# Block passes over w1 with 512-column products, sums of weights for four steps at a time, and other PSUM banks

## The chip, the cores and the metric

The kernel runs on one core of one Trainium2 chip. The metric is device time in microseconds (us). The kernel before takes 515.64 us (median of 3 runs, 515.21 to 515.76).

## The reference

A transformer block on S = 2048 tokens with D = 512 channels: a linear-attention mixer, and then an MLP over the token axis. The change lies in the MLP:

```python
h  = x + attention(layernorm(x))
g  = layernorm(layernorm(h))            # (S, D)
u  = gelu(einsum("sd,sf->df", g, w1) + b1)   # w1 (2048, 1792)
y  = einsum("df,fs->ds", u, w2) + b2         # w2 (1792, 2048)
out = h + y.T
```

## The kernel before

**Passes and steps.** The hidden axis F = 1792 is cut into 7 passes of 256. Passes 0 and 1 are multiplied during the attention's last turns. From then on an explicit list, `STEPS`, orders the work: steps 0 to 7 are pass 2, a plain pass ("v"); steps 8 to 31 are passes 3, 4 and 5, the block passes ("u"); steps 32 to 39 are pass 6, plain again; steps 40 to 95 are w2's ("y"), seven steps for each pair of output tiles. A step of w1 takes two tiles of 128 tokens against 256 columns of w1.

**Block passes.** A plain step does four 128x128 blocks of weights against 512 columns, with three matmuls each: high part of the weights by high part of the data, high by low, low by high. A block step is a Strassen-like scheme with seven products (`P1` to `P7`) in place of eight. It needs, on 256 columns, sums of weight blocks (`w_sums`) and sums of data blocks (made by `h_ops`, split into high and low parts by `h_parts` into tiles named `cb`; step 8 + j uses data pair j).

**From weight to matmul.** For each step, SP loads raw blocks into one half of a double buffer (`BLOCK`, four steps in each half); DVE makes four sums in place (`w_sums`, L801 to L805); then `w_parts` splits the step's seven blocks: ACT copies them to the high part (L66, 128x896) and DVE subtracts that to get the low part (L67, 128x896). In w1's steps the parts of step n lie in one of three buffers, `ws[n % 3]`, so that the copy of step n + 3 has to wait until TensorE has finished step n. The loop calls `prepare(n + 2)` while step n is issued. Before, `w_sums` does two steps at a time in w1's passes, behind the parts of every even step m, for steps m + 2 and m + 3.

**Order.** From the attention's end on, ACT, DVE, POOL, PE and SP run in the order in which the code issues (`manual_schedule`). The calls put down with `at(n, ...)` come behind `prepare(n + 2)`, at half steps ahead of it: `h_sums` (four DVE adds for one data pair), `h_parts`, `u_adds` (ACT copies and accumulating DMAs that POOL issues, at the steps in `U_ADDS`), `u_parts` (ACT and DVE splits of a finished pass's u, for w2).

**Banks.** `ps_b` has four PSUM banks, `ps_f` and `ps_q` two each. Before, a block pass takes four banks (`four_banks`): pass 3 and 5 two of `ps_f` and two of `ps_q`, pass 4 four of `ps_b`; the plain pass 6 takes two of `ps_b`. `u_out` reads a finished pass out of its banks into u. The steps of w2 already use four products of 512 columns (`wide`) and three of 256 (`narrow`), in six banks.

Of the kernel before, what the change touches and what calls it, by code (L numbers as in the profile page):

```python
# [9 lines left out]
F32 = mybir.dt.float32  # L10
# [7 lines left out]
P = 128  # L18
# [24 lines left out]
def block_kernel(ctx: ExitStack, tc: tile.TileContext, x, xT, wT, phic, wo, w1, b1, w2, b2,  # L43
# [749 lines left out]
    def w_sums(g):  # L793

        if 2 * g >= len(STEPS) or STEPS[2 * g][0] == "v":
            return
        plain = STEPS[2 * g][0] == "y"
        raw = BLOCK[g // 2 % 2] if plain else RAW[g]
        added = ADDED(2 * g)
        if not added:  # L800
            nc.vector.tensor_add(raw[:, :, 0], raw[:, :, 3], raw[:, :, 1])  # L801
        nc.vector.tensor_add(raw[:, :, 5], raw[:, :, 0], raw[:, :, 2])
        nc.vector.tensor_add(raw[:, :, 6], raw[:, :, 4], raw[:, :, 5])
        if not added:
            nc.vector.tensor_add(raw[:, :, 1], raw[:, :, 1], raw[:, :, 2])  # L805
# [199 lines left out]

    def four_banks(i):
        return [new_bank(q) for q in ((ps_b,) * 4, (ps_f, ps_f, ps_q, ps_q))[i]]
# [7 lines left out]
    def firsts(banks):  # L1015
        a, b, c, d = banks
        tmp = wqp.tile([P, 4, HD], F32, name="tmp", tag="small")
        nc.scalar.activation(tmp[:, 1], a[:, 0], AF.Copy)
        nc.vector.tensor_sub(tmp[:, 2], a[:, 1], tmp[:, 1])
        nc.vector.tensor_sub(tmp[:, 3], tmp[:, 2], d[:, 0])  # L1020
        nc.vector.scalar_tensor_tensor(tmp[:, 0], b[:, 0], -1.0, tmp[:, 2], op0=ALU.mult, op1=ALU.subtract)
        return tmp[:, 0:2], tmp[:, 3].unsqueeze(1).to_broadcast([P, 2, HD])

    def u_out(p, banks):
        e, u3 = firsts(banks)
        U[p] = o = ur.tile([P, 4, HD], F32, name="u")
        nc.vector.tensor_add(o[:, 0:2], banks[1], u3)
        nc.vector.tensor_add(o[:, 2:4], banks[2], e)

# [11 lines left out]
    def wide_step(n, sp, p):  # L1041
        t = 2 * sp
        if p == 0:
            b3, b2 = [new_bank((ps_f, ps_q)[sp % 2]) for _ in range(2)]
            BK[:] = [new_bank(ps_b) for _ in range(4)] + [b3, b2]
# [46 lines left out]
    def last_step(n, sp, p):  # L1092
        t = 2 * sp
        if p == 0:
            b3, b2 = [new_bank((ps_f, ps_q)[sp % 2]) for _ in range(2)]
            BK[:] = [new_bank(ps_b) for _ in range(4)] + [b3, b2]
# [46 lines left out]
    def step(n):  # L1143

        kind, i, j = STEPS[n]
        if kind == "u":
            if j == 0:
                BANKS[0] = four_banks(i % 2)
            products(n, BANKS[0], lambda m: NB[j][m], j == 0, j == NT // 2 - 1)
# [4 lines left out]
        elif kind == "v":  # L1154
            if j == 0:
                PU[i] = [ps_b.tile([P, D], F32, name="pu", tag="pu") for _ in range(2)]
            wh_, wl_ = PARTS[n]
# [58 lines left out]
    def prepare(m):  # L1216
# [82 lines left out]
```

## Time and profile before

| what | value |
|---|---|
| time, median of 3 | 515.64 us |
| span of the profiled execution, first to last instruction | 513.1 us |
| PE busy in the span | 507.8 us (99%) |
| DVE, ACT, POOL busy | 438.4, 310.6, 261.1 us |
| block passes (steps 8 to 31), 288.47 to 348.94 us: DVE, ACT busy | 55.28, 37.70 us of 60.47 |
| granted TensorE clock | 1.000 |

The profiled execution has only its span; the time of a run is about 2.5 us longer than this (515.64 - 513.1), for what lies ahead of the first and behind the last instruction. In the rows of a timeline the first column is the start from the span's beginning, the second the duration (of a group: to the end of its last), and the brackets hold the engine's idle time just before and who ended it. A row "x9" is nine of the same kind in sequence.

### The profile page before, as it was taken

To read this page: it belongs to the slowest core of one execution; us is meant where nothing else is said; L and a number is where in the kernel's file an instruction comes from. 1 tells how busy PE (TensorE), PEld (TensorE's weight loads), DVE (VectorE), ACT (ScalarE), POOL (GpSimd) and SP (SyncE) were. 2 spreads that over 40 slices of the span, in tenths; PEclk is the share of its full clock that TensorE was granted. 3 is DMA by queue.
4 is the path that set the end of the run, shared out by engine and by line. 5 is a ranking of instruction groups with operands and counts; after the bars stand their busy time and mean duration, and the time that the engine had idled before them with its cause. 6 is when DMAs were issued, how large, how long until landed. Compare 5 with 4: busy or idle time off the path is not lost.

```text
span 513.1 us, 10496 instructions
## 1 busy us (share of the span) xinstructions
PE 507.8 (99%) x4024; PEld 441.7 (86%) x4024; DVE 438.4 (85%) x746; ACT 310.6 (61%) x557; POOL 261.1 (51%) x212
## 2 busy tenths in 40 slices
PE   8999999999999999999999999999999999999997
PEld 8888888888877777777788999998899999999997
DVE  6799889989887899699877898898799889868983
ACT  6999863525267878867676754577655444434530
POOL 3579997876999999985200421202323212211220
PEclk9999999999999999999999999999999999999999
DMA  8642301010123234354325775545677797668734
GB/s 308 217 144 84 103 22 42 1 65 21 42 64 103 67 100 145 127 169 132 95 69 185 150 159 125 133 115 151 173 164 147 181 199 167 122 153 190 169 51 85
DMA packets 53266, 63.35 MB, mean 123 GB/s; under 512 B 4832, under 2 KB 39904, under 8 KB 53216
## 3 DMA queue, kind: packets, MB, share of 16 engines
q1 hardware_dynamic: 44288, 51.90, 32.5%
q0 software_dynamic: 8640, 10.62, 14.9%
q8 instruction: 31, 0.51, 0.4%
q10 hardware_dynamic: 288, 0.17, 0.1%
q14 instruction: 19, 0.16, 0.1%
HBM read 48.39 MB, written 11.14 MB: 116 GB/s over the span
## 4 chain that ended last, share of the span: by engine, by line
PE 95%; DVE 2%; ACT 1%; DMA 1%; issue 0%; POOL 0%; DVEq 0%
PE py L989 25%; PE py L996 9%; PE pu L71 9%; PE pu L72 8%; PE pu L73 8%; PE py L998 4%; PE pk_ps L71 3%; PE pk_ps L72 3%; PE pk_ps L73 3%; PE pv L73 3%; PE pv L71 3%; PE pv L72 3%; PE po L71 3%; PE po L73 2%; PE po L72 2%; PE pn L616 2%
## 5 line engine op out<-in xcount | busy, mean ns | idle before, releaser
L66 ACT ACTIVATE wp<-wraw 128x896 fp32r<-128x896 f32 (+1 forms) x96 | 82.4, 895 | 68.3 <-DVE wraw L805 23.9
L67 DVE TENSOR_TENSOR wp<-wraw,wp 128x896 fp32r<-128x896 f32 (+1 forms) x96 | 95.5, 1019 | 14.9 <-ACT wp L66 14.6
L989 PE MATMUL py<-cb,wp 128*128 128x256 f32 x678 | 92.6, 283 | 0.0
L989 PEld LDWEIGHTS py<-cb,wp 128*128 128x128 f32 x678 | 86.1, 191 | 0.0
L1039 POOL DMA_DIRECT2D out<-u x28 | 24.8, 963 | 89.8 <-ACT u L1085 28.9
L951 POOL DMA_DIRECT2D tt<-u x14 | 13.4, 960 | 60.6 <-ACT tt L950 34.5
L490 POOL TENSOR_TENSOR ez<-eq,zB 128x1024 f32<-128x1024 f32 x16 | 38.4, 2406 | 3.8 <-ACT zB L550 3.8
L219 POOL TENSOR_TENSOR pk<-pk,sk 128x1024 f32<-128x1024 f32 x16 | 31.1, 1947 | 11.3 <-DVE sk L218 10.1
L996 PE MATMUL py<-cb,wp 128*128 128x512 f32 x126 | 36.1, 394 | 0.0
L514 POOL TENSOR_TENSOR eq<-eq,w 128x1024 f32<-128x1024 f32 x16 | 32.4, 2025 | 3.5 <-DVE w L511 3.5
L223 POOL TENSOR_TENSOR zacc<-zacc,pk 128x1024 f32<-128x1024 f32 x13 | 31.4, 2412 | 0.5
L989 PE MATMUL py<-hs,wp 128*128 128x256 f32 x216 | 30.0, 283 | 0.0
L989 PEld LDWEIGHTS py<-hs,wp 128*128 128x128 f32 x216 | 27.8, 192 | 0.1
L195 ACT ACTIVATE pk<-pk,r 128x1024 f32<-128x1024 f32 x16 | 18.4, 1149 | 15.0 <-DVE pk L173 14.4
L989 PE MATMUL py<-uf,wp 128*128 128x256 f32 x198 | 26.6, 283 | 0.0
L71 PE MATMUL pu<-wq,xs 128*128 128x512 f32 x64 | 26.1, 409 | 0.0
L71 PE MATMUL pu<-hs,whl 128*128 128x512 f32 x64 | 26.0, 406 | 0.0
L71 PE MATMUL po<-woh,oh 128*128 128x512 f32 x64 | 25.3, 396 | 0.1
L72 PE MATMUL pu<-wq,xs 128*128 128x512 f32 x64 | 25.0, 391 | 0.0
L73 PE MATMUL pu<-wq,xs 128*128 128x512 f32 x64 | 25.0, 390 | 0.0
L72 PE MATMUL pu<-hs,whl 128*128 128x512 f32 x64 | 25.0, 390 | 0.0
L73 PE MATMUL po<-woh,ol 128*128 128x512 f32 x64 | 25.0, 390 | 0.0
(226 smaller groups left out, 1422.1 us busy)
## 6 DMA issues: line engine op xcount, KB each, us to landing
wraw<-in_w SPq DMA_DIRECT2D x112, 256.0 KB, 3.4
out<-u POOLq DMA_DIRECT2D x21, 256.0 KB, 5.4
xraw<-in_xT SPq DMA_DIRECT2D x16, 256.0 KB, 2.9
xh<-in_x SPq DMA_DIRECT2D x16, 256.0 KB, 2.7
h<-in_x SPq DMA_DIRECT2D x16, 256.0 KB, 2.9
out<-h SPq DMA_DIRECT2D x16, 256.0 KB, 2.0
wraw<-in_wT SPq DMA_DIRECT2D x12, 256.0 KB, 4.9
tt<-u POOLq DMA_DIRECT2D x14, 128.0 KB, 3.8
```

The costliest lines, as they stand in the source:

```text
L66: nc.scalar.activation(hi, src, AF.Copy)
L67: lo_engine.tensor_sub(lo, src, hi)
L71: nc.tensor.matmul(o, ah, bh, start=first, stop=False)
L72: nc.tensor.matmul(o, ah, bl, start=False, stop=False)
L73: return nc.tensor.matmul(o, al, bh, start=False, stop=last).ins
L219: nc.gpsimd.tensor_mul(heads(PK[t]), heads(PK[t]), sk.unsqueeze(2).to_broadcast([P, 2 * H, DH]))
L223: nc.gpsimd.tensor_add(zacc, zacc, PK[t])
L490: nc.gpsimd.tensor_mul(EZ[t], EQ[t], zB)
L514: nc.gpsimd.tensor_mul(heads(EQ[t]), heads(EQ[t]), W[t].rearrange("p g c h -> p (g c h)").unsqueeze(2).to_broadcast([P, 2 * H, DH]))
L989: nc.tensor.matmul(o, w[:, m[0]], x[:, y], start=opens and i == 0, stop=closes and i == 2, skip_group_check=True)
L996: nc.tensor.matmul(o, wh_[:, m[0]], x(m[1]), start=first, stop=False, skip_group_check=True)
L1039: nc.gpsimd.dma_start(out[t * P:(t + 1) * P, k * HD:], flat(a), accum_op=ALU.add)
```

## The change

It does four things.

1. `products` (the block steps of w1) does P3, P2, P5 and P4 by `wide`: one matmul of 512 columns for the weights' high part (data high and low side by side) and one of 256 for the low part, 17 matmuls in place of 21. A pass now takes six banks (`six_banks`): always the four of `ps_b`, and two of `ps_q` (passes 3 and 5) or `ps_f` (pass 4). The order of the products differs in a pass's first, middle and last steps. `u_out` now has five ACT copies out of the banks (before: one) and nine DVE operations (before: five).
2. `w_sums` in w1's passes does four steps at a time, behind the parts of step m where m % 4 is 3, for steps m + 1 to m + 4 (those of steps 12 to 15 behind the parts of step 11, and so on).
3. The plain pass 6 takes `ps_f`; w2's pairs take `ps_q` and `ps_f` in the other order.
4. `U_ADDS` shifts eight calls of `u_adds` by a step (pass 0's last two, pass 1's last two, all of pass 2, one of pass 3), and the adds and parts of data pair 6 come a step later.

```diff
-        plain = STEPS[2 * g][0] == "y"
-        raw = BLOCK[g // 2 % 2] if plain else RAW[g]
+        raw = BLOCK[g // 2 % 2]
...
-    U_ADDS = {0: (5, 7, 9), 1: (6, 8, 10), 2: (11, 13, 15), 3: (19, 21, 23), 4: (28, 30, 32), 5: (34, 35.5, 37)}
+    U_ADDS = {0: (5, 8, 10), 1: (6, 9, 11), 2: (12, 14, 16), 3: (19, 21, 24), 4: (28, 30, 32), 5: (34, 35.5, 37)}
...
+    def six_banks(pool):
+        b3, b2 = [new_bank(pool) for _ in range(2)]
+        return [new_bank(ps_b) for _ in range(4)] + [b3, b2]
 
     def products(n, banks, x, first, last):
-        a, b, c, d = banks
-        for o, m, opens in ((a[:, 0], P1, True), (a[:, 1], P6, False), (d[:, 0], P7, True), (b[:, 0], P5, True),
-                            (b[:, 1], P4, False), (c[:, 0], P3, True), (c[:, 1], P2, False)):
-            narrow(o, n, m, x(m[1]), first and opens, last)
+        b16, b7, b5, b4, b3, b2 = banks
+
+        def singles():
+            narrow(b16[:, 0], n, P1, x(P1[1]), first, last)
+            narrow(b16[:, 1], n, P6, x(P6[1]), False, last)
+            narrow(b7[:, 0], n, P7, x(P7[1]), first, last)
+
+        w3, w2, w5, w4 = (b3, P3), (b2, P2), (b5, P5), (b4, P4)
+        if last:
+            singles()
+            wide(n, x, first, last, w5, w4)
+            wide(n, x, first, last, w3, w2)
+        elif first:
+            wide(n, x, first, last, w3, w2)
+            singles()
+            wide(n, x, first, last, w5, w4)
+        else:
+            wide(n, x, first, last, w3, w2, w5, w4)
+            singles()
...
+    def u_out(p, banks):
+        b16, b7, b5, b4, b3, b2 = banks
         tmp = wqp.tile([P, 4, HD], F32, name="tmp", tag="small")
+        u3, e0, e1, u2 = [tmp[:, k] for k in range(4)]
         U[p] = o = ur.tile([P, 4, HD], F32, name="u")
+        add, sub = nc.vector.tensor_add, nc.vector.tensor_sub
+        nc.scalar.activation(e1, b16[:, 0], AF.Copy)
+        for k, b in enumerate((b5, b4, b3, b2)):
+            nc.scalar.activation(o[:, k], b[:, 1], AF.Copy)
+        sub(u2, b16[:, 1], e1)
+        sub(u3, u2, b7[:, 0])
+        add(o[:, 0], b5[:, 0], o[:, 0])
...
-    for j, n in enumerate((0, 1, 2, 3, 5, 9, 12), 1):
+    for j, n in enumerate((0, 1, 2, 3, 5, 10, 12), 1):
...
-        elif m % 2 == 0 and m + 2 < Y0:
+        elif m % 4 == 3 and m + 1 < Y0:
             w_sums(m // 2 + 1)
```

How the rows of DVE stand at the first block pass. `wp<-wraw,wp` is the low part of one step, `wraw<-wraw` a sum of weights, `hf<-hf` the adds for a data pair, `cb_3571` the parts of data pair 6. Before, from the low part of step 10 on:

```order
L67 TENSOR_TENSOR wp<-wraw,wp 128x896
L801 TENSOR_TENSOR wraw<-wraw 128x2x128
L802 TENSOR_TENSOR wraw<-wraw 128x2x128
L803 TENSOR_TENSOR wraw<-wraw 128x2x128
L805 TENSOR_TENSOR wraw<-wraw 128x2x128
L67 TENSOR_TENSOR wp<-wraw,wp 128x896
L67 TENSOR_TENSOR cb_3571<-hf,cb_3571 128x4x256
L67 TENSOR_TENSOR wp<-wraw,wp 128x896
```

These are the low part of step 10, the sums for steps 12 and 13, the low part of 11, the parts of pair 6, the low part of 12. Now, from the low parts of steps 8 to 10 on:

```order
L67 TENSOR_TENSOR wp<-wraw,wp 128x896 x3
L738 TENSOR_TENSOR hf<-hf 128x256 x2
L739 TENSOR_TENSOR hf<-hf 128x256 x2
L67 TENSOR_TENSOR wp<-wraw,wp 128x896
L800 TENSOR_TENSOR wraw<-wraw 128x4x128
L801 TENSOR_TENSOR wraw<-wraw 128x4x128
L802 TENSOR_TENSOR wraw<-wraw 128x4x128
L804 TENSOR_TENSOR wraw<-wraw 128x4x128
L67 TENSOR_TENSOR wp<-wraw,wp 128x896
L67 TENSOR_TENSOR cb_3571<-hf,cb_3571 128x4x256
L738 TENSOR_TENSOR hf<-hf 128x256 x2
L739 TENSOR_TENSOR hf<-hf 128x256 x2
```

Between the low parts of steps 10 and 11 stand the adds of pair 6; between those of 11 and 12 stand the sums for steps 12 to 15, twice as wide; behind 12 come the parts of pair 6 and the adds of pair 7, and then the low part of step 13.

DVE at the end of that pass (step 15), now: the low part of step 15, the sums for steps 16 to 19, the low parts of 16 and 17, and the first four operations of `u_out`, which read the banks of pass 3 (`py`):

```order
L67 TENSOR_TENSOR wp<-wraw,wp 128x896
L800 TENSOR_TENSOR wraw<-wraw 128x4x128
L801 TENSOR_TENSOR wraw<-wraw 128x4x128
L802 TENSOR_TENSOR wraw<-wraw 128x4x128
L804 TENSOR_TENSOR wraw<-wraw 128x4x128
L67 TENSOR_TENSOR wp<-wraw,wp 128x896 x2
L1039 TENSOR_TENSOR tmp<-py,tmp 128x256
L1040 TENSOR_TENSOR tmp<-tmp,py 128x256
L1041 TENSOR_TENSOR u<-py,u 128x256
L1042 TENSOR_TENSOR u<-py,u 128x256
```

Before, the sums for steps 18 and 19 stood between the low parts of 16 and 17, and no matmul of step 16 wrote into a bank that `u_out` was still to read.

PE at the same seam, now, with what its rows wait for: the end of step 15 (first two rows), and step 16:

```order
L995 MATMUL py<-hs,wp 128x512 x2
L997 MATMUL py<-hs,wp 128x256 x2
L995 MATMUL py<-hs,wp 128x512 [waits Activation_49]
L995 MATMUL py<-hs,wp 128x512
L997 MATMUL py<-hs,wp 128x256 [waits DVE_49]
L997 MATMUL py<-hs,wp 128x256
L988 MATMUL py<-hs,wp 128x256 [waits DVE_49]
L988 MATMUL py<-hs,wp 128x256 x2
L988 MATMUL py<-cb_3447,wp 128x256 x3
L988 MATMUL py<-cb_3447,wp 128x256 [waits DVE_49]
```

The first 512-column matmul waits for ACT (the high part of step 16), the first with low weights (L997) for DVE (the low part), and the first of P1 (L988) for DVE again: it opens the bank that `u_out` reads with its first two operations.

More of the change, by code (lines that the diff above doesn't have):

```diff
@@ new lines, in u_out @@
+    def u_out(p, banks):
+        b16, b7, b5, b4, b3, b2 = banks
+        tmp = wqp.tile([P, 4, HD], F32, name="tmp", tag="small")
+        u3, e0, e1, u2 = [tmp[:, k] for k in range(4)]
+        U[p] = o = ur.tile([P, 4, HD], F32, name="u")
+        add, sub = nc.vector.tensor_add, nc.vector.tensor_sub
[5 more added lines that the diff above has]
+        add(o[:, 0], b5[:, 0], o[:, 0])
+        add(o[:, 1], b4[:, 0], o[:, 1])
+        nc.vector.scalar_tensor_tensor(e0, o[:, 0], -1.0, u2, op0=ALU.mult, op1=ALU.subtract)
+        add(o[:, 0], o[:, 0], u3)
+        add(o[:, 2], b3[:, 0], o[:, 2])
+        add(o[:, 3], b2[:, 0], o[:, 3])
+        add(o[:, 1:4], o[:, 1:4], tmp[:, 0:3])
@@ L1043, in wide_step @@
         if p == 0:
-            b3, b2 = [new_bank((ps_f, ps_q)[sp % 2]) for _ in range(2)]
+            b3, b2 = [new_bank((ps_q, ps_f)[sp % 2]) for _ in range(2)]
             BK[:] = [new_bank(ps_b) for _ in range(4)] + [b3, b2]
@@ L1094, in last_step @@
         if p == 0:
-            b3, b2 = [new_bank((ps_f, ps_q)[sp % 2]) for _ in range(2)]
+            b3, b2 = [new_bank((ps_q, ps_f)[sp % 2]) for _ in range(2)]
             BK[:] = [new_bank(ps_b) for _ in range(4)] + [b3, b2]
@@ L1147, in step @@
             if j == 0:
-                BANKS[0] = four_banks(i % 2)
+                BANKS[0] = six_banks((ps_f, ps_q)[i % 2])
             products(n, BANKS[0], lambda m: NB[j][m], j == 0, j == NT // 2 - 1)
@@ L1155, in step @@
             if j == 0:
-                PU[i] = [ps_b.tile([P, D], F32, name="pu", tag="pu") for _ in range(2)]
+                PU[i] = [(ps_f if i > PLAIN else ps_b).tile([P, D], F32, name="pu", tag="pu") for _ in range(2)]
             wh_, wl_ = PARTS[n]
```

13 lines of the change are left out of this document (removed).

## The prediction

> **What bounds the kernel now.** I read the page's busy shares first, then who waited for whom on PE, and then the chain that ended last.
>
> ```profile
> PE 507.8 (99%) x4024; PEld 441.7 (86%) x4024; DVE 438.4 (85%) x746; ACT 310.6 (61%) x557; POOL 261.1 (51%) x212
> PE pk_ps L357 <- DVE eps L62: 1.1, 1, 1.1
> PE pu L335 <- POOL ph L361: 0.4, 1, 0.4
> PE pn L616 <- DVE h L641: 0.2, 1, 0.2
> PE 95%; DVE 2%; ACT 1%; DMA 1%; issue 0%; POOL 0%; DVEq 0%
> ```
>
> The middle three rows are all the waits of PE: 1.7 us, none in the steps that change. So PE's own stream sets the time, and a change counts if it shortens that stream or puts a wait into it. The chain gives the block passes in one piece, and a middle step of w2 in three:
>
> ```profile
> 288.63 60.47 PE py L989 x504
> ...
> 397.00 1.07 PE py L989 x9
> 398.07 0.93 PE py L996 x4
> 399.00 0.47 PE py L998 x4
> ```
>
> 504 matmuls are 24 steps of 21: 120 ns each, 2.52 us per step, with no gap. w2's step, which has the new form already, takes 1.07 + 0.93 + 0.47 = 2.47 us.
>
> The second view is how full the other engines are there (columns: stretch, its length, then busy PE, PEld, DVE, ACT, POOL):
>
> ```profile
> 288.47:348.94 60.47, 60.47 (x505) 60.47 (x504) 55.28 (x92) 37.70 (x57) 13.84 (x16) 1.00 0.60 139
> 303.83 0.96 ACT L66 ACTIVATE wp<-wraw 128x896 fp32r<-128x896 f32 x1 [0.67 <-PE py L989]
> 306.35 0.95 ACT L66 ACTIVATE wp<-wraw 128x896 fp32r<-128x896 f32 x1 [1.56 <-PE py L989]
> 302.86 1.24 PE L989 MATMUL py<-hs,wp 128*128 128x256 f32 x9
> 305.38 1.24 PE L989 MATMUL py<-hs,wp 128*128 128x256 f32 x9
> ```
>
> DVE is busy for 91% of the block passes. The copies of steps 16 and 17 begin 0.25 us after steps 13 and 14 have ended (a step begins 0.72 us into a row of nine: 303.58, 306.10), because there are only three buffers of parts. So the parts can never be far ahead of PE, and DVE has little to catch up with.
>
> **What the change takes away.** Per step 0.05 us of PE, 24 times: 1.15 us. The Trainium skill, in "TensorE: Matmul & The Clock Gate", Back-to-back issue gap, prices a warm matmul at its columns over 2.4 GHz plus 2.5 ns; by that the twelve old and the eight new matmuls differ in four times 2.5 ns, 0.24 us in all, as an estimate. The rows disagree (120 ns for 256 columns, 0.93 / 4 = 233 ns for 512), and I go by them.
>
> **What it puts in.** Sums of four steps at a time exist in w2's part; there the rows show what follows them:
>
> ```profile
> 371.94 0.69 DVE L801 TENSOR_TENSOR wraw<-wraw 128x512 f32<-128x512 f32 x1
> ...
> 374.01 0.68 DVE L805 TENSOR_TENSOR wraw<-wraw 128x512 f32<-128x512 f32 x1
> 375.76 1.09 DVE L67 TENSOR_TENSOR wp<-wraw,wp 128x896 fp32r<-128x896 f32 x1 [1.07 <-ACT wp L66]
> 374.77 0.95 ACT L66 ACTIVATE wp<-wraw 128x896 fp32r<-128x896 f32 x1 [2.89 <-issue]
> ```
>
> Four sums take 2.75 us; the copy of the next step can begin only after them, and DVE stands idle for 1.07 us until its low part can follow. For two steps they took 1.68 us:
>
> ```profile
> 306.00 0.42 DVE L801 TENSOR_TENSOR wraw<-wraw 128x256 f32<-128x256 f32 x1
> ...
> 307.26 0.42 DVE L805 TENSOR_TENSOR wraw<-wraw 128x256 f32<-128x256 f32 x1
> ```
>
> They served steps further on, so that the next step's copy ran beside them. DVE thus saves 0.61 us for four steps and loses 1.07. In w2 more buffers cover that; in w1 nothing does. I follow DVE's rows in the new order from a place that stays as it was, the low part of step 10:
>
> ```profile
> 290.23 1.09 DVE L67 TENSOR_TENSOR wp<-wraw,wp 128x896 fp32r<-128x896 f32 x1 [0.37 <-ACT wp L66]
> 293.83 1.22 DVE L67 TENSOR_TENSOR cb<-hf,cb 128x1024 fp32r<-128x1024 f32 x1
> 297.56 0.88 DVE L738 TENSOR_TENSOR hf<-hf 128x256 f32<-128x256 f32 x2
> 298.47 0.89 DVE L739 TENSOR_TENSOR hf<-hf 128x256 f32<-128x256 f32 x2
> 299.27 2.08 DVE L67 TENSOR_TENSOR wp<-wraw,wp 128x896 fp32r<-128x896 f32 x2
> 308.60 0.42 DVE L1019 TENSOR_TENSOR tmp<-py,tmp 128x256 f32<-128x256 f32 x1
> ...
> 310.39 0.68 DVE L1028 TENSOR_TENSOR u<-py,tmp 128x512 f32<-128x512 f32 x1
> 302.45 0.40 ACT L950 ACTIVATE u<-u 128x256 f32<-128x256 f32 x1
> 288.47 0.52 PE L989 MATMUL py<-hs,wp 128*128 128x256 f32 x3
> ```
>
> Low 10 ends at 291.3. Adds of pair 6 (1.8 us): 293.1. Low 11 (1.0 behind other work): 294.1. Sums for 12 to 15 (2.75): 296.8. Copy, then low 12 (0.07 + 0.95, 0.03 + 1.09): 298.9. Parts of pair 6 (1.15): 300.0. Adds of pair 7: 301.7. Low 13: 302.7. PE begins step 8 at 288.47 and would begin step 12 at 298.36 and step 13 at 300.83. A middle step wants its low part 0.93 us after its start, behind its four 512-column products: 299.29 for step 12, met with 0.3 to spare; 301.76 for step 13, **missed by 1.0 us**, with 0.1 for the signal.
>
> On to the seam. Low 14: 303.7. Parts of pair 7: 304.8. Low 15: 305.8. Sums for 16 to 19: 308.5. Low 16: 310.6. Copy 17 stands behind two ACT copies of `u_adds` (0.3 each), so low 17 ends at 312.1. Only then comes `u_out`'s first subtraction (0.42): 312.4. Step 16 would begin at 309.25 and, 0.70 us later (two products of 512, two of 256), open the bank which that subtraction reads. It can at 312.5 in place of 309.95, **2.55 us** late. Before, passes alternated between banks, and nothing waited here.
>
> The same chain at the later places, with 2.47 us per step: step 18 begins at 316.75, `u_out` ends at 316.0, low 19 at 317.9, sums at 320.6, low 20 at 322.7 against 322.6 wanted: **0.2**. Copy 23 starts 0.25 behind step 20; low 23 ends at 326.7, sums 329.3, low 25 at 332.5, `u_out`'s first at 332.8 against 332.5: **0.4** at step 24's bank. Step 28 repeats step 20: **0.2**. Behind low 28 stand the parts of pass 0's u:
>
> ```profile
> 338.80 0.95 DVE L67 TENSOR_TENSOR cb<-tt,cb 128x768 fp32r<-128x768 f32 x1
> 339.66 2.09 DVE L67 TENSOR_TENSOR wp<-wraw,wp 128x896 fp32r<-128x896 f32 x2
> 341.67 1.22 DVE L67 TENSOR_TENSOR cb<-u,cb 128x1024 fp32r<-128x1024 f32 x1
> 362.58 1.83 DVE L67 TENSOR_TENSOR wp<-wraw,wp 128x896 fp32r<-128x896 f32 x2 [1.02 <-ACT wp L66]
> ```
>
> 1.22 + 0.95 more, so low 29 is **0.5** late. In plain pass 6, the third `u_out` (nine operations, 3.9 us by the 0.42 and 0.95 of these rows, for the 2.5 from L1019 to L1028) puts DVE back just ahead of the sums for step 40, which already end in a stand-still of 1.02 us; step 38 may lose **0.4** (0 to 0.8). The waits sum to 1.0 + 2.55 + 0.2 + 0.4 + 0.2 + 0.5 + 0.4 = 5.25 us. Less 1.15 that is **4.1 us more**: span 513.1 to 517.2. The time of a run is 2.5 us above the span, so 515.64 becomes **519.8 us**.
>
> **What I cost at nothing.**
>
> ```profile
> 387.53 0.38 ACT L1080 ACTIVATE u<-py 128x256 f32<-128x256 f32 x1 [0.67 <-PE py L998]
> 296.72 0.42 ACT L950 ACTIVATE tt<-wraw 128x256 f32<-128x256 f32 x1 [2.01 <-DMA wraw<-u]
> ```
>
> The four more copies of ACT per `u_out` (0.38 each, as in w2's steps) lie beside DVE, and ACT is busy for 37.70 of 60.47 us; uncovered they would cost 1.5 us per pass. The moved `u_adds` issue the same DMAs on POOL in nearly the same order, now behind other ACT copies; ACT's waits for landings were no wait of PE. Uncovered, a late one holds a copy by up to 2.0 us. Pass 6 in `ps_f` finds free banks as it did in `ps_b`; in `ps_b` it would now wait like step 16. SP's loads keep their order, each behind the low part eight steps earlier.
>
> **Rivals.**
>
> *The chain on DVE does not bind: faster.* If copies 12 and 16 ran beside the sums, as before, DVE would gain 1.07 us at each, and with 1.0 us less neither step 13 nor, mostly, the bank of step 16 would wait. Then only 1.15 us go: 514.5. It decides at 1.0 us of slack between low 10 and low 13. Against it stands the idle 1.07 in w2's row, on the same two lines. Chance 0.10.
>
> *Half of it.* The waits of step 13 and of the seam overlap more, or low parts are wanted later than I say, and 1 to 2.5 us of waits stay: 515.5 to 517.0. Chance 0.12, two thirds of it within 0.2% (1.0 us, about what a measurement of this kernel can tell from no change).
>
> *Only columns count.* Old and new forms stream the same 3072 columns for four products. If these set the pace, the 1.15 us don't come and the waits do: 520.9. w2's steps speak against it. Chance 0.06. The gap rule of the Trainium skill above is nearly this one; by it the time would be 520.6.
>
> *PE runs slowly after a wait.* At the start of the trace it does, for one kind of 128x128 fp32 matmul after another:
>
> ```profile
> L357 PE MATMUL pk_ps<-ones 128*128 128x128 f32 x18 | 3.7, 392 | 1.1 <-DVE eps L62 1.1
> L335 PE MATMUL pu<-ph,wraw 128*128 128x128 f32 x16 | 2.1, 285 | 0.4 <-POOL ph L361 0.4
> ```
>
> 3.7 / 18 = 206 ns each, then 131. A stretch of 3.7 us at that rate loses 3.7 x (1 - 131 / 206) = 1.35 us; after the waits of steps 16 and 13 it would be 521.1 to 522.5. Chance 0.07, since the single waits are short (1.0 and 1.6 us). The Trainium skill, same page, What's actually happening, says that the clock halves after about 3.4 us of idleness and comes back after as long a busy stretch; by it no wait here is long enough, and the first rows fit the second half of the rule.
>
> **Numbers.** Forecast 0.65, with a range of its own of 518.6 to 521.2 (seven waits, each 0.2 us uncertain for the signal and the weight load behind it, and 0 to 0.8 at step 38). Faster by over 0.2%: 0.10. Within: 0.07. Slower: 0.83. The range 516.5 to 522.5 leaves out the first rival, most of the second, and little above.
>
> **What would show it.** Right: rows of PE waiting for DVE `wp` L67 and for `tmp` L1039, the longest near 310 us; DVE idle for about 1.07 us ahead of the low parts of steps 12, 16, 20, 24, 28; no PE wait ahead of step 13; w2's steps and the granted clock as before. Wrong: block passes of 59.3 us without PE waits (first rival), or waits in other places, for ACT or for DMA.

## The result, and the profile after

The changed kernel takes **523.05 us** (median of 4 runs, 520.86 to 523.65) where the kernel before takes 515.70 beside it: ratio **1.0137, interval 1.0116 to 1.0157**. The forecast was 519.8. Its sign held, its size did not: 4.1 us were forecast and 7.35 came, above both ranges that went with the forecast (518.6 to 521.2, and 516.5 to 522.5). Of the four executions one kept the granted clock throughout (mean 1.000) and took 520.86 us; the other three, at a mean of 0.997, took 522.74 to 523.65. The profiled execution has a span of 521.0 us, 7.9 more than before. One execution of the kernel e13 below, 1287.12 us with every matmul slow, is left out of that kernel's ratio. Line numbers below are those of the kernel named; in the changed kernel the narrow products are L988 and the wide ones L995 and L997.

First the page of the changed kernel: PE's busy time, and the clock granted to it in 40 slices of the span.

```profile
PE 512.3 (98%) x3928; PEld 438.6 (84%) x3928; DVE 440.5 (85%) x734; ACT 312.9 (60%) x569; POOL 261.1 (50%) x212
PEclk9999999999999999999999998999999999999999
```

PE has 96 matmuls fewer and is busy 4.5 us longer. One slice of the clock shows an 8: something slowed the matmuls themselves, and no wait list can show that. The waits of PE and of its weight loads (in total, times, longest):

```profile
PE py L997 <- DVE wp L67: 1.7, 3, 1.0
PE py L988 <- DVE tmp L1039: 1.6, 2, 1.3
PE py L988 <- DVE u L1097: 0.4, 1, 0.4
PEld py L997 <- DVE wp L67: 3.3, 4, 1.4
```

Where the time went is read from stretches that are the same work in both kernels: the block passes, plain pass 6, and the first and second quarter of w2 (stretch, length, then busy PE, PEld, DVE, ACT, POOL and the clock). First the kernel before, whose block passes the prediction has shown (60.47):

```profile
348.94:370.73 21.79, 21.79 (x99) 18.03 (x97) 16.73 (x26) 14.60 (x28) 5.02 (x6) 1.00 0.60 146
370.73:406.38 35.65, 35.65 (x246) 33.13 (x245) 31.98 (x50) 18.90 (x33) 10.37 (x13) 1.00 0.81 179
406.38:441.93 35.55, 35.55 (x248) 33.07 (x246) 32.22 (x49) 16.31 (x26) 7.32 (x9) 1.00 0.74 160
```

The changed kernel:

```profile
288.90:355.21 66.31, 62.92 (x409) 56.47 (x408) 55.64 (x79) 39.77 (x68) 13.80 (x17) 0.97 0.55 128
355.21:377.40 22.19, 22.19 (x99) 17.87 (x97) 18.30 (x32) 13.92 (x29) 4.46 (x7) 1.00 0.58 139
377.40:413.35 35.95, 35.95 (x247) 33.26 (x245) 32.28 (x49) 20.29 (x35) 11.15 (x14) 1.00 0.75 174
413.35:449.80 36.45, 36.03 (x247) 33.20 (x246) 32.24 (x50) 16.28 (x26) 8.09 (x10) 1.00 0.78 166
```

The block passes take 5.84 us more, plain pass 6 takes 0.40, w2's first quarter 0.30, its second 0.90; the parts ahead of the block passes began 0.43 later, and the rest of w2 is the same to 0.02. The two places in the block passes that the prediction named are there. DVE, from step 12's low part to the seam (start, duration, and in brackets the idle time ahead):

```profile
298.36 1.09 DVE L67 TENSOR_TENSOR wp<-wraw,wp 128x896 fp32r<-128x896 f32 x1 [1.16 <-ACT wp L66]
...
302.22 2.08 DVE L67 TENSOR_TENSOR wp<-wraw,wp 128x896 fp32r<-128x896 f32 x2
...
310.26 1.09 DVE L67 TENSOR_TENSOR wp<-wraw,wp 128x896 fp32r<-128x896 f32 x1 [1.16 <-ACT wp L66]
311.71 1.09 DVE L67 TENSOR_TENSOR wp<-wraw,wp 128x896 fp32r<-128x896 f32 x1 [0.36 <-ACT wp L66]
312.72 0.42 DVE L1039 TENSOR_TENSOR tmp<-py,tmp 128x256 f32<-128x256 f32 x1
```

PE at the same places:

```profile
303.36 0.39 PE L997 MATMUL py<-hs,wp 128*128 128x256 f32 x1 [1.01 <-DVE wp L67]
...
311.40 0.50 PE L997 MATMUL py<-hs,wp 128*128 128x256 f32 x2 [0.40 <-DVE wp L67]
313.19 0.78 PE L988 MATMUL py<-hs,wp 128*128 128x256 f32 x3 [1.28 <-DVE tmp L1039]
```

The brackets on DVE are the stand-still of sum, copy and low part: 1.16 us, forecast 1.07 (1.16 also ahead of steps 20, 24 and 28). The brackets on PE count from the modelled end of the matmul before; counted from start to start, step 13 loses 1.27 us and step 16 loses 2.52: 0.41 at its first products, whose weight load waits for ACT's copy, 0.67 at the low part and 1.44 at the bank. And then comes what the forecast did not have:

```profile
310.07:313.49 3.42, 1.59 (x7) 0.90 (x7) 2.77 (x4) 3.42 (x10) 1.75 (x2) 1.00 0.34 55
313.49:316.90 3.41, 3.41 (x15) 3.12 (x14) 3.34 (x9) 0.80 (x3) 0.00 (x0) 0.50 0.74 176
316.90:320.31 3.41, 3.41 (x24) 3.10 (x23) 3.34 (x5) 2.07 (x4) 0.86 (x1) 1.00 0.45 89
```

For 3.41 us after the wait the clock was granted at 0.50, and 15 matmuls were done where the next equal stretch did 24. By the starts of the matmuls that costs 1.60 us.

### The profile page after: what moved, and what is told of

It reads as the page before. It is cut to its first block, busy times and chain, and to the rows that moved or that the text cites. A ratio compares the mean times of both kernels' runs of the same rounds, so it can differ in the third digit from the quotient of the medians.

```text
span 521.0 us, 10300 instructions
## 1 busy us (share of the span) xinstructions
PE 512.3 (98%) x3928; PEld 438.6 (84%) x3928; DVE 440.5 (85%) x734; ACT 312.9 (60%) x569; POOL 261.1 (50%) x212
## 3 DMA queue, kind: packets, MB, share of 16 engines
HBM read 48.39 MB, written 11.14 MB: 114 GB/s over the span
## 4 chain that ended last, share of the span: by engine, by line
PE 84%; DVE 9%; ACT 3%; issue 2%; DMA 1%; DVEq 0%; ACTq 0%
PE py L988 15%; PE py L995 9%; PE pu L71 8%; PE pu L73 8%; PE pu L72 8%; PE py L997 5%; DVE wp L67 3%; PE pk_ps L71 3%; PE pk_ps L72 3%; PE pk_ps L73 3%; PE pv L73 3%; PE pv L72 3%; PE pv L71 3%; PE po L71 3%; PE po L73 2%; PE po L72 2%
## 5 line engine op out<-in xcount | busy, mean ns | idle before, releaser
L988 PE MATMUL py<-cb,wp 128*128 128x256 f32 x534 | 75.9, 284 | 0.4 <-DVE u L1097 0.4
L988 PEld LDWEIGHTS py<-cb,wp 128*128 128x128 f32 x534 | 69.3, 192 | 0.6 <-DVE u L1097 0.6
L995 PE MATMUL py<-cb,wp 128*128 128x512 f32 x174 | 51.9, 399 | 0.0
L995 PEld LDWEIGHTS py<-cb,wp 128*128 128x128 f32 x174 | 30.0, 191 | 4.0
L997 PEld LDWEIGHTS py<-cb,wp 128*128 128x128 f32 x174 | 28.8, 190 | 4.1
L997 PE MATMUL py<-cb,wp 128*128 128x256 f32 x174 | 31.3, 281 | 0.0
L988 PE MATMUL py<-uf,wp 128*128 128x256 f32 x198 | 26.7, 283 | 0.0
L71 PE MATMUL pu<-wq,xs 128*128 128x512 f32 x64 | 26.1, 409 | 0.0
L71 PE MATMUL pu<-hs,whl 128*128 128x512 f32 x64 | 25.9, 405 | 0.0
L988 PEld LDWEIGHTS py<-uf,wp 128*128 128x128 f32 x198 | 25.0, 191 | 0.1
L71 PE MATMUL pu<-hs,wp 128*128 128x512 f32 x64 | 25.0, 391 | 0.0
L73 PE MATMUL pu<-hs,wp 128*128 128x512 f32 x64 | 25.0, 391 | 0.0
```

The costliest lines, as they stand in the source:

```text
L71: nc.tensor.matmul(o, ah, bh, start=first, stop=False)
L73: return nc.tensor.matmul(o, al, bh, start=False, stop=last).ins
L988: nc.tensor.matmul(o, w[:, m[0]], x[:, y], start=opens and i == 0, stop=closes and i == 2, skip_group_check=True)
L995: nc.tensor.matmul(o, wh_[:, m[0]], x(m[1]), start=first, stop=False, skip_group_check=True)
L997: nc.tensor.matmul(o[:, 0], wl_[:, m[0]], x(m[1])[:, 0], start=False, stop=last, skip_group_check=True)
```

## The experiments

My theory was that of the prediction (PE loses time wherever DVE's serial chain is late), with two additions from the trace: that the idle PE of step 16 drew a clock of 0.5, and that DVE comes late into w2 too. Fifteen kernels take the change apart (five), test the clock (three), test w2 (three) and try to keep the gain (four). Each ratio is against the kernel before on the same chip, whose median was 515.3 to 515.6.

### The change taken apart

**Sums of two, all else of the change** (e1_sums_of_two).

```diff
-        raw = BLOCK[g // 2 % 2]
+        raw = BLOCK[g // 2 % 2] if STEPS[2 * g][0] == "y" else RAW[g]
...
-        elif m % 4 == 3 and m + 1 < Y0:
+        elif m % 2 == 0 and m + 2 < Y0:
```

> The changed kernel with the sums of weights for two steps at a time again, all else as changed. My theory (the chain on DVE of four sums, copy and low part over three buffers of parts makes PE wait): DVE's idle 1.07 us ahead of the low parts of steps 12, 16, 20, 24, 28 goes, and with it the waits at steps 20, 24, 28, 29; the adds of pair 6, which now stand behind the low part of step 10, and the bank of step 16 still cost about 0.4 + 0.4 + 1.0 us at steps 13, 15 and 16; with 1.15 us less matmul time that is 516.0 to 517.0 us, and TensorE keeps its full clock. Rival (the reuse of the same four banks at the seams is the cause): the wait at step 16 stays at 2.5 us with the drop of the clock behind it, 519 or more. Rival (the shifted adds of pair 6 are the cause): no change against the changed kernel at step 13, 520 or more.

Measured: 517.61 us (516.13 to 522.34), ratio 1.0041 (1.0019 to 1.0063). That is 0.6 above my range and well under the rivals'. So some 5 of the 7.35 us need the sums of four. The block passes took 61.55 us, near the 60.47 of before. The profiled execution was the slowest: it lost 3.29 us in w2 in one wait for `u` L1098, and the clock fell after it. The other nine, at a mean clock of 0.999 or 1.000, took 516.13 to 518.25 us.

**Sums of four alone, in the kernel before** (e2_four_alone): the diff above, the other way round.

> The kernel before with one part of the change alone: sums of weights for four steps at a time. My theory in its simple form (sums of four cost PE 1 us or more by themselves): 517 or more. By the same hand-made chain with the old products, the old place of pair 6's adds and the steps of 2.52 us, every low part still comes in time or within 0.05 us of it (steps 16, 20 and 29 are at the edge), so that the sums of four alone would cost 0 to 0.5 us: 515.6 to 516.2, and the cost arises only together with the other parts. Rival (banks or clock): 515.7, with slack left at steps 16, 20, 28.

Measured: 515.73 us (515.54 to 516.58), ratio 1.0006 (0.9996 to 1.0015). No wait of PE stands in its list that is not there before, but the list leaves out the smallest: by the starts of the matmuls 0.2 us are lost at each of steps 16, 20 and 29, and the profiled block passes take 61.14 us, 0.67 more. So the sums of four cost little by themselves: 0.3 us by the medians, which the interval doesn't tell from nothing.

**Wide products and six banks alone** (e5_wide_and_banks): sums of two, `U_ADDS` and pair 6 as before.

> The kernel before with the 512-column products and the six banks alone (sums of two, u_adds and pair 6 where they were). My theory: the bank of step 16 is read by u_out just in time (0 to 0.3 us of wait), no low part is late, and the 1.15 us of matmul time come through: 514.5 to 515.0, faster than both kernels. Rival (banks at the seams are the cause): 2.5 us or more at step 16, 517 or more. Rival (only columns count, the 512-column form gains nothing): 515.7 to 516.0, with block steps of 2.52 us.

Measured: 515.98 us (514.81 to 517.69), ratio 1.0009 (0.9996 to 1.0022). Neither part costs by itself what both cost together, but the gain did not come either. Block passes and plain pass of this kernel:

```profile
288.80:349.19 60.39, 60.13 (x410) 55.23 (x409) 57.20 (x98) 40.21 (x66) 12.92 (x16) 1.00 0.58 136
349.19:371.36 22.17, 22.17 (x99) 17.87 (x98) 18.28 (x32) 13.93 (x29) 4.49 (x7) 1.00 0.59 141
```

60.39 stands where 60.47 - 1.15 = 59.32 was due. By the starts of the matmuls 0.23 us are lost at the bank of step 16, 0.30 at that of step 24 and 0.49 at step 29's low part; then 0.38 in the plain pass and 0.57 in w2. DVE is busy for 57.20 us of these passes, 55.28 before.

**Pair 6 back at 9** (e3_pair6_back): the changed kernel with one number as before.

```diff
-    for j, n in enumerate((0, 1, 2, 3, 5, 10, 12), 1):
+    for j, n in enumerate((0, 1, 2, 3, 5, 9, 12), 1):
```

> The kernel after with one number of its tables as before: the sums and parts of pair 6 at 9, not 10. My theory: each PE wait is where the serial chain of VectorE ends late, so pair 6 is what step 13 waits for. Its 1.27 us go, the step-16 wait falls from 2.5 to about 1.6 us, and with so little idle in one place the half-clock stretch after it (1.6 us) goes as well: 523.05 - 1.27 - 0.9 - 1.6 = 519.3, range 518.5 to 520.0, no stretch at a granted clock of 0.5 in the profile. Rival A, any wait over 1.3 us halves the clock: the stretch stays, 520.9. Rival B, the place of pair 6 doesn't matter because the sums of four alone make the waits: 522.5 to 523.5.

Measured: 519.79 us (519.27 to 520.11), ratio 1.0083 (1.007 to 1.0096). Waits of PE:

```profile
PE py L988 <- DVE tmp L1039: 1.6, 2, 1.3
PE py L995 <- ACT wp L66: 0.6, 1, 0.6
PE py L997 <- DVE wp L67: 0.3, 1, 0.3
```

Step 13's wait is gone, step 16 loses 1.88 us, and the clock stays at 1.00 throughout. One number of a table is worth about 3 us. The second row is new, at step 20, where 1.07 us are lost: the changed kernel lost nothing there, because PE came later.

**Both tables of places back** (e6_adds_and_pair6_back): wide products, six banks and sums of four are left.

> The kernel after with both tables of places as before (U_ADDS and pair 6), so that the wide products, the six banks and the sums of four are left of the change. My theory: as for pair 6 alone, and the step-16 wait falls by a further 0.4 us to 1.2: 518.9, range 518.0 to 519.7, no half-clock stretch. Rival: the moved adds were what kept ScalarE free for the copies of weights, and without them the waits grow: 520.5 or more.

Measured: 518.55 us (517.90 to 522.40), ratio 1.0075 (1.0052 to 1.0097). Step 16 loses 1.43 us, the block passes take 62.75. So the wide form and the sums of four together cost 3.0 us where alone neither costs anything that its interval tells from none: the first puts four DVE operations more at each seam, the second holds DVE up for 2.75 us and a copy just ahead of it. The moved places added some 4 us to that.

### The clock

**Something to do in the wait** (e4_fill_the_wait): the changed kernel with seven extra 512-column matmuls ahead of step 16's own, into a bank that the step opens next and so overwrites.

```diff
         elif first:
+            for _ in range(7 if n == 16 else 0):
+                nc.tensor.matmul(b3, CB[0][:, 0, 0, 0:P], x(0), start=True, stop=True, skip_group_check=True)
             wide(n, x, first, last, w3, w2)
             singles()
```

> The changed kernel with seven idle matmuls of 512 columns (1.63 us) ahead of step 16's first product, into the bank that this product opens anyway. They add 1.63 us of PE work where PE would wait for 2.5 us. If the half clock seen for 3.4 us behind this wait comes from the idleness, it goes in all runs and the time falls by about 1.6 us, to 520.9 to 521.5, as in the one run of the changed kernel at full clock (520.86). If the slow stretch has another cause (contention at the banks, say), it stays and the time is unchanged or up to 1 us longer: 523 to 524.

Measured: 521.12 us (520.38 to 521.40), ratio 1.0102 (1.0084 to 1.0119), 1.9 us under the changed kernel, or 1.65 when each is counted from the kernel before on its own chip. The stretch that holds the wait, and the one after it:

```profile
309.88:313.29 3.41, 2.64 (x14) 2.06 (x13) 2.79 (x4) 3.41 (x10) 1.75 (x2) 1.00 0.32 44
313.29:316.70 3.41, 3.41 (x25) 3.15 (x24) 3.34 (x9) 0.77 (x3) 0.00 (x0) 1.00 0.79 192
```

The waits for DVE are as late as they were; PE, kept busy, keeps its clock. The slow stretch came of the idleness.

**One long wait in the kernel before** (e8_one_long_wait): DVE held up at one place by the same add done 19 times.

```diff
-            nc.vector.tensor_add(raw[:, :, 0], raw[:, :, 3], raw[:, :, 1])
+            for _ in range(19 if g == 11 else 1):
+                nc.vector.tensor_add(raw[:, :, 0], raw[:, :, 3], raw[:, :, 1])
```

> The kernel before with the first add of the weights' sums of steps 22 and 23 done 19 times over (same operands, same result): VectorE is held up by 18 x 0.35 = 6.2 us at one place, so the low part of step 22 comes 2.0 to 2.3 us after PE needs it, in one wait. Theory (an idle PE of 2 us or more within a few us halves the clock): a stretch at granted clock 0.5 follows and costs 1.6 to 1.9 us: 519.0 to 519.8. Rival (only an idleness of 3 us and over does it, and the stretch of the kernel after came of something else): no stretch, 517.3 to 517.9.

Measured: 524.18 us (one run). I had the repeated add at 0.35 us; it takes 0.46, each waiting for the one before, so the wait was 5.46 us.

```profile
320.51:323.92 3.41, 1.52 (x13) 1.31 (x11) 3.17 (x8) 0.00 (x0) 0.00 (x0) 1.00 0.03 3
323.92:327.34 3.42, 0.02 (x1) 0.02 (x1) 3.22 (x8) 0.99 (x2) 0.00 (x0) 0.50 0.00 0
327.34:330.75 3.41, 3.41 (x16) 3.41 (x17) 3.34 (x6) 1.42 (x3) 1.75 (x2) 0.50 0.47 125
330.75:334.16 3.41, 3.41 (x30) 3.41 (x30) 1.96 (x4) 1.15 (x2) 0.00 (x0) 1.00 0.84 182
```

The clock falls in the middle of the wait, 2.1 us after PE stopped, and is back one stretch after PE resumed. In each kernel whose clock fell (this one, the changed one, e1, e9 and e10) the fall comes a whole number of 3.413 us after the clock's first rise (93, 90, 119, 106 and 96 of them), so the stretches are a fixed grid.

**A shorter wait** (e11_shorter_wait): the same with 12 adds.

> As e8_one_long_wait (the kernel before with the first add of the sums of steps 22 and 23 repeated), with 12 adds in place of 19, each 0.46 us: one wait of PE of 5.5 - 7 x 0.46 = 2.3 us at step 22. Theory: the clock is set in stretches of 3.41 us that follow one another without a gap, and is halved for one stretch when PE idled more than about 1.7 to 1.95 us within the stretch ahead of it; so there is a stretch at 0.5 if 1.95 us or more of the wait falls into one of them, and none if the wait is cut by a boundary into two parts under 1.66 us. 519.4 with a stretch, 517.7 without. Rival (what counts is the length of the wait, wherever the boundaries lie, with a limit between 1.7 and 2.5 us): a half stretch begins right at the wait's end or there is none, whatever the boundaries.

Measured: 517.51 us (one run), a wait of 2.24 us, and no slow stretch. The grid cut it in two:

```profile
319.26:322.67 3.41, 2.66 (x23) 2.45 (x21) 3.17 (x9) 0.00 (x0) 0.00 (x0) 1.00 0.25 38
322.67:326.08 3.41, 2.08 (x17) 2.09 (x18) 3.28 (x6) 2.40 (x4) 0.60 (x1) 1.00 0.24 70
```

A single wait of 2.24 us left the clock alone, while waits of together 2.5 us, none of them over 1.5 and nearly all within one stretch, cost the changed kernel 1.6 us. What decides is how much of a stretch PE is busy, not the longest wait.

### w2 and the plain pass

**The kernel before with the new outputs' load** (e7_before_with_outputs_load): at each seam four ACT copies and four DVE adds more, whose results the old sums overwrite.

```diff
+        for k, b in enumerate((banks[1][:, 0], banks[1][:, 1], banks[2][:, 0], banks[2][:, 1])):
+            nc.scalar.activation(o[:, k], b, AF.Copy)
+        for k, b in enumerate((banks[1][:, 0], banks[1][:, 1], banks[2][:, 0], banks[2][:, 1])):
+            nc.vector.tensor_add(o[:, k], b, o[:, k])
         nc.vector.tensor_add(o[:, 0:2], banks[1], u3)
```

> The kernel before (narrow products, its own banks, sums of two) with only the load of the new output added: at the end of each block pass four more copies on ScalarE and four more 256-column adds on VectorE, whose results are overwritten by the sums that stood there. Nothing of the result changes. My theory: w2 and the plain pass lose time after the change because VectorE, with about 1.7 us more at each pass's end, comes into them 1 us later, so that the loads, which follow its low parts, are later too: 0.4 to 1.0 us over before, 515.8 to 516.4. Rival: w2's loss is of its own bank pools, which the change swaps: 515.4, within 0.2 of before.

Measured: 518.19 us (517.43 to 520.54), ratio 1.0065 (1.0048 to 1.0083): 2.7 us, not 0.4 to 1.0. Block passes and w2's first quarter:

```profile
288.81:350.98 62.17, 61.36 (x506) 60.72 (x505) 57.73 (x99) 39.71 (x65) 13.61 (x16) 1.00 0.59 135
372.79:409.30 36.51, 36.20 (x247) 33.21 (x246) 32.89 (x51) 20.43 (x35) 11.89 (x14) 1.00 0.75 173
```

The load costs 1.7 us in the block passes, which I had not expected, and 0.86 in w2's first quarter. The second quarter stays at 35.55. The kernel overstates the load somewhat: a seam's outputs hold DVE for 4.62 us here, 0.72 of it idle behind the copies, for 4.06 in the changed kernel and 2.47 before. Most telling is when w2's loads are issued, counted from w2's first matmul: the one at +15.16 us before comes at +16.67 here, at +16.59 in e5 and at +16.63 in the changed kernel. So the outputs' work alone is enough to make w2's loads as late as they are in the changed kernel, with the old order of the banks. The rival, the swapped banks, falls for this lateness and for the first quarter. For the second quarter no run settles it (see below).

**First sums of w2 by transfers** (e9_banks_added_w2_start): e5 with accumulating transfers of POOL for two of four sums of steps 40 to 43.

```diff
-        return n in () or n - Y0 in range(8, 16)
+        return n in () or n - Y0 in (0, 1, 2, 3, 8, 9, 10, 11, 12, 13, 14, 15)
```

> The kernel e5_wide_and_banks (wide products and six banks, sums of two, every place as before), in which the first two of the four sums of w2's first four steps are made by POOL's accumulating transfers instead of VectorE, as the kernel does for other steps of w2: VectorE has 1.4 us less to do just ahead of w2. My theory: of e5's 1.15 us of gain, 0.95 us are given back in the plain pass and in w2 because VectorE comes into them 1.1 to 1.4 us later; then most of these 0.95 us come back: 0.5 to 1.0 us under e5, so 0.1 to 0.6 us under before (514.9 to 515.4 where before is 515.5). Rival: these losses come of how the transfers land, whose time VectorE doesn't set, and two more accumulating transfers make it worse: 516.0 or more.

Measured: 521.25 us (520.86 to 522.91), ratio 1.0119 (1.0102 to 1.0136). The rival's range is met, but by a wait that neither side named:

```profile
PE pu L71 <- ACT wp L66: 4.0, 1, 4.0
```

The copy of step 38 stands on ACT behind that of step 40, which waits for the sums, and these for the transfers. Though DVE had less to do, PE lost 4.19 us at once and the clock after it. w2's first quarter then took 35.65 as before, but PE came to it more than 4 us later, so this doesn't show that less work on DVE did it.

**The same for steps 28 to 31 too** (e10_added_also_pass_five).

> The same, and the first two sums of steps 28 to 31 by accumulating transfers too: VectorE has 1.7 us less to do ahead of step 29, where e5 waited 0.49 us for a low part. Theory (VectorE's lateness is what PE waits for): a further 0.3 to 0.5 us under the kernel above. Rival (POOL's queue, which also carries the accumulating adds of the pairs, becomes the late one): slower than the kernel above by 0.3 us or more, with PE waiting for parts of the pairs.

Measured: 523.76 us (523.71 to 525.86), ratio 1.0167 (1.0154 to 1.0181): a second wait of 3.39 us, at the bank of step 24, and 2.5 us more than e9 where my theory had less. Two of its stretches sit close to the clock's limit: PE busy for 1.80 us in each, and the clock kept after the first and halved after the second:

```profile
368.30:371.72 3.42, 1.80 (x8) 1.15 (x7) 1.38 (x2) 0.53 (x1) 0.00 (x0) 1.00 0.19 28
371.72:375.13 3.41, 1.80 (x7) 1.20 (x8) 2.77 (x3) 3.41 (x7) 1.77 (x2) 1.00 0.20 42
375.13:378.54 3.41, 3.41 (x10) 2.64 (x9) 1.72 (x3) 0.79 (x3) 0.00 (x0) 0.50 1.06 240
```

### Tries to keep the gain

**Two places moved in e5** (e12_banks_two_places), **and the same in the kernel before** (e13_before_two_places).

```diff
-    U_WORK = {0: 26, 1: 28, 2: 30, 3: 32, 4: 34, 5: 38, 6: 41}
+    U_WORK = {0: 27, 1: 28, 2: 30, 3: 32, 4: 34, 5: 38, 6: 41}
...
+        if n == Y0 - 5:
+            w_sums(Y0 // 2)
-        while ahead <= n + 5 and n not in HELD and (n < Y0 or STEPS[n][2] != NP - 2):
-            if ahead in (Y0, Y0 + 4):
+        while ahead <= n + 5 and n > Y0 - 5 and n not in HELD and (n < Y0 or STEPS[n][2] != NP - 2):
+            if ahead == Y0 + 4:
```

> The kernel e5_wide_and_banks with two places moved: the parts of pair 0 come one step later (27, not 26), behind the low part that step 29 waits for, and the weights' sums of w2's first four steps stay where they are while the copy and low part of w2's first step come one step later, behind those of step 38. Theory (PE waits where VectorE's serial chain is late): e5's waits of 0.49 at step 29 and 0.30 to 0.38 in the plain pass go, and some of w2's 0.57 with them: 514.7 to 515.2 where before is 515.4, so under the kernel before by 0.2 to 0.7 us. Rival (the lateness moves on to the next low part or to w2's loads, since VectorE's work stays the same): no change against e5, 515.7 to 516.2.

> The kernel before with the same two places moved and nothing else. Theory: PE of the kernel before waits for none of these parts, so nothing changes: within 0.2 us of before. Rival (the places themselves save time, for instance in w2): as much under before as the kernel above is under e5.

Measured: 516.52 us (515.61 to 519.43), ratio 1.0018 (1.0003 to 1.0033), and for e13 515.37, ratio 0.9994 (0.9985 to 1.0003; ten of its executions 514.95 to 516.11). Both waits of e5 did go, though 0.30 us appear at step 31 instead: block passes 60.14, plain pass 21.77. But w2 gave 1.6 us away, the first quarter 0.5 and the second 1.1:

```profile
407.28:443.91 36.63, 36.06 (x248) 33.21 (x246) 32.89 (x51) 16.31 (x26) 8.77 (x10) 1.00 0.81 168
```

**Only the first of the two places** (e15_banks_one_place).

> The kernel e5_wide_and_banks with only the parts of pair 0 a step later (27). Theory: the 0.49 us at step 29 go, nothing else does, and w2 loses as in e5 (0.57): 515.4 to 515.7 where before is 515.5. Rival: what is gained at step 29 is lost again in w2 (as in e12, which lost 1.6 us there), 515.8 to 516.6; then w2's loss doesn't hang on the place of w2's first parts, but on how its transfers fall.

Measured: 516.11 us (515.00 to 517.07), ratio 1.0009 (0.9998 to 1.0020). Step 29's wait is gone (block passes 60.09), w2 loses 1.1 us. The rival is nearer.

**Pass 5 narrow again, passes 3 and 4 wide** (e14_last_pass_narrow; pass 5 with the old `products` and `u_out` in two banks of `ps_q` and the first two of `ps_b`, and the parts of pair 0 at 27).

> The kernel e5_wide_and_banks with pass 5, the last block pass, in the old form (narrow products into four banks, the old sums of its outputs), and the parts of pair 0 a step later (27). The wide form stays in passes 3 and 4, 16 steps: a gain of 16 x 0.048 = 0.77 us. Theory: w2 and the plain pass lose time because the outputs of the last wide pass put about 1.7 us more on VectorE just ahead of them. Then plain pass and first half of w2 take what they take before (21.79, 35.65, 35.55 us), the loads of w2 are issued as early as before, only the seam at step 16 loses 0.2 to 0.3 us, and the time is 514.7 to 515.1 where before is 515.5. Rival: VectorE's load of the two earlier passes reaches w2 as well, since little of it is caught up: w2 loses 0.5 us or more and the time is 515.4 to 516.2.

Measured: 515.69 us (514.94 to 518.63), ratio 1.0002 (0.9988 to 1.0016).

```profile
348.73:370.52 21.79, 21.79 (x99) 18.02 (x98) 16.77 (x29) 13.50 (x26) 4.94 (x7) 1.00 0.62 151
370.52:406.17 35.65, 35.65 (x247) 33.14 (x246) 32.11 (x49) 19.78 (x34) 10.49 (x13) 1.00 0.75 169
406.17:442.51 36.34, 36.06 (x248) 33.20 (x247) 32.73 (x51) 16.30 (x26) 8.24 (x10) 1.00 0.77 168
```

Plain pass and first quarter are those of before to 0.01 us: their losses came of the last wide pass, most likely of its outputs, whose work alone cost e7 0.86 in that quarter. The second quarter still loses 0.79 and the rest of w2 0.25, and the load that was issued at +15.16 us before comes at +16.14. So the time is that of the rival: some of the lateness comes from the two earlier passes.

What happens there is the same in all kernels. At the seam of the third pair of w2, DVE does the weights' sums ahead of the pair's outputs, and the sums wait for one load. Before, and in the changed kernel:

```profile
417.14 0.69 DVE L801 TENSOR_TENSOR wraw<-wraw 128x512 f32<-128x512 f32 x1 [0.29 <-DVE wp L67]
```

```profile
426.74 0.69 DVE L800 TENSOR_TENSOR wraw<-wraw 128x512 f32<-128x512 f32 x1 [2.42 <-issue]
...
430.41 0.42 DVE L1097 TENSOR_TENSOR u<-py,u 128x256 f32<-128x256 f32 x1
```

The brackets don't name the load, but in both kernels the sum begins 0.08 us after it has landed. It is one load in each kernel. From issue to landing it takes 3.4 us in the kernel before and 5.5 in the changed one (size of the transfer in KB, then us to landing):

```profile
wraw<-in_w SPq DMA_DIRECT2D x1, 256.0 KB, 3.4
```

```profile
wraw<-in_w SPq DMA_DIRECT2D x1, 256.0 KB, 5.5
```

Just ahead of it POOL issues two stores of outputs. In us from w2's start, in order of the load's landing:

| kernel | load issued | second store lands | load lands | loss of the quarter |
|---|---|---|---|---|
| before | 42.98 | 45.69 | 46.33 | 0 |
| e2 | 42.98 | 45.56 | 46.76 | 0.00 |
| e11 | 42.94 | 47.69 | 48.04 | 0.01 |
| e3 | 44.14 | 47.88 | 48.22 | 0.13 |
| e9 | 43.32 | 46.33 | 48.31 | 0.31 |
| e7 | 43.80 | 48.00 | 48.39 | 0.00 |
| e5 | 43.81 | 47.93 | 48.60 | 0.30 |
| e14 | 43.66 | 49.03 | 48.83 | 0.79 |
| e10 | 42.94 | 48.60 | 48.98 | 0.94 |
| e15 | 44.02 | 48.45 | 49.14 | 0.63 |
| e4 | 44.23 | 48.50 | 49.19 | 0.73 |
| changed | 43.79 | 48.80 | 49.26 | 0.90 |
| e12 | 44.26 | 49.02 | 49.62 | 1.08 |
| e6 | 44.33 | 49.27 | 49.69 | 1.19 |

The loss roughly follows the landing, and the issue does not decide alone: in e10 and e11 it comes as early as before. What goes with the landing is the second store: the load lands 0.3 to 0.7 us after it, except in e2, e9 and e14. In e11, whose only edit is the add repeated in step 22's sums, the store is late and the load with it. So the likely cause of the late landing is that the stores, when late, fly beside the load; a kernel in which only the stores move was not tried, and this stays open. Open too is what the banks add: the kernels with the old order of w2's banks (before, e2, e7, e11) lose nothing here, and none of them has a landing after 48.39. Against the banks as the cause stands the code: the bank that PE waits for at 430.88 is one of `ps_b`, whose order in w2 the change leaves as it was.

No version beats the kernel before. The wide form's 1.15 us are there in PE's stream, and every arrangement that was tried gives them back.

## Why the prediction was off

- **PE is the bound, and the wide step gains 1.15 us:** right. e5's block passes take 60.39 us with 1.02 of waits in them, so 59.37 without; forecast 59.32. The rival in which only columns count falls.
- **Four sums, a copy, a low part in series, and DVE idle ahead of steps 12, 16, 20, 24 and 28:** right in mechanism and place, 1.16 us instead of 1.07. The rival in which the chain doesn't bind falls with it.
- **The waits, one by one** (forecast, then measured from start to start): step 13: 1.0, 1.27. Step 16: 2.55, 2.52. Step 20: 0.2, 0. Step 24: 0.4, 0.55. Step 28: 0.2, 0.43. Step 29: 0.5, 0.53. Step 38: 0.4, 0.36. In sum 5.25 and 5.66. Following DVE by hand through thirty steps gave six of the seven places and nearly each size; step 20 lost nothing. Pair 6 as what step 13 waits for is shown by e3.
- **"w2's steps and the granted clock as before":** the clock is the step that failed first. The rival of a slow PE after a wait was there, but with a chance of 0.07, "since the single waits are short". The single waits didn't matter; their sum within 3.41 us did. It cost 1.6 us by the matmuls and 1.65 to 1.9 by e4; the one execution that kept its clock, at 520.86 us, lies in the forecast's narrower range. The Trainium skill, in "TensorE: Matmul & The Clock Gate", What's actually happening, has a free-running window of 4096 cycles at 1.2 GHz, 3.41 us, and a halved clock after an idle window. The trace agrees with the length and the grid. It differs from how the prediction used the rule, as if PE had to be idle for all of 3.4 us: here 1.59 us of work in a window of 3.41 did not save the clock. The window's grid and the sum of waits in it were the question to ask.
- **The same line's w2, and pass 6's 0.4 as the end of the lateness:** the step that failed second, 1.2 us. The third `u_out` was followed only to step 38. Its lateness (forecast 1.4 us more work, measured 1.6) went on through DVE's low parts into the loads of w2, which are issued 0.8 us late and more as far as the third pair's seam, and it came back as a load that landed 49 us into w2 and a wait of PE 3.5 us behind it. e7 shows the lateness, e14 that the first quarter's loss and the plain pass's come of the last wide pass. Why the load then takes longer is open, but for the stores beside it.
- **What I cost at nothing, the extra copies and adds of `u_out` beside DVE:** not free in general. In e7, where no sums of four stand, they cost 1.7 us in the block passes. In the changed kernel the gain, the waits and the slow clock account for the block passes to 0.1 us, so there the term is no separate part of the miss.

The terms add up: -1.15 of gain, 5.30 of waits in the block passes, 1.60 of slow clock, 0.40 in pass 6, 1.20 in w2 and 0.43 ahead of the block passes (kernels whose code is unchanged up to there show from -0.10, e15, to +0.74, e12) make 7.78 of the span's 7.9 us. The times differ by less, 7.35: a run of the changed kernel is 1.7 us longer than its span (522.74 and 521.0), not the 2.5 that were taken over from the kernel before.

## What to carry to other kernels

Where an engine beside the bound is busy for nine tenths of a stretch, price a change by the work it puts on that engine first: 1.15 us off PE were paid for with 1.6 us on DVE (4.06 for 2.47) at each of three seams, and a lateness that nobody catches up travels on to whatever follows, here to loads 50 us later. When waits come close together, add them up within the window in which the clock is decided, since a second loss as large as the waits can follow. And take a change apart in both directions: the wide products and the sums of four each cost next to nothing alone, 3.0 us together, and 7 with the moved places, of which one number in a table made 3.

## What the runs showed of the hardware

The clock of PE is decided per stretch of 3.413 us on a fixed grid, and a stretch in which PE is busy for less than about half is followed by one at 0.50:

| kernel, stretch | PE busy of 3.41 us | clock in the next |
|---|---|---|
| e8, 320.51 | 1.52 | 0.50 |
| changed, 310.07 | 1.59 | 0.50 |
| e1, 409.90 | 1.64 | 0.50 |
| e10, 371.72 | 1.80 | 0.50 |
| e10, 368.30 | 1.80 | 1.00 |
| e11, 510.40 | 1.86 | 1.00 |
| e8, 412.67 | 2.00 | 1.00 |
| e1, 406.49 | 2.06 | 1.00 |
| e11, 322.67 | 2.08 | 1.00 |

These are the stretches nearest to the limit. It lies near 1.8 us by these columns, whose matmul ends are modelled. A stretch in which PE is busy throughout brings the clock back at once; by the starts of the matmuls such a slow stretch cost 1.5 to 1.6 us in each of the five kernels, and by e4 1.65 to 1.9 in the changed one. So equal waits can cost differently by where they fall on the grid, which the program doesn't set: one of the changed kernel's four executions kept its clock.
